# Scatters one per step, gates behind the row sums, and half blocks on 128 columns of weights, in a gated linear attention with a top-1 router

## The chip, the cores and the metric

The kernel runs on one core of one Trainium2 chip. The metric is the time of one execution on the device in microseconds (us); of several runs the median counts.

## The reference

All arrays are float32. For 4 batches and 8 heads of width 48, over 768 steps:

```python
state = alpha[:, :, t, :, None] * state + np.einsum('bhd,bhe->bhde', k[:, :, t], v[:, :, t])
y[:, :, t] = np.einsum('bhd,bhde->bhe', q[:, :, t], state)
```

The result, as 3072 token rows x of 384 numbers, goes through a router with 8 experts:

```python
logits = (x / norm(x)) @ (expert_emb / norm(expert_emb)).T / tau
expert_idx = argmax(logits); gate_w = softmax(logits)[expert_idx]
h = np.maximum(x[mask] @ w1[e], 0.0)              # w1: 384 x 1024
out[mask] = gate_w[mask, None] * (h @ w2[e])      # w2: 1024 x 384
```

Each token goes through the one expert that it chose.

## The kernel before, in words

**First stage: attention and routing.** The 3072 tokens are 24 chunks of 128 (six for each batch), and a loop at L719 takes one chunk per step, with work of earlier chunks in the same step. Step s loads chunk s + 2 (`load`, L447, on the SP queue), turns its alpha, k and q on TensorE and scans the decays on VectorE (`decays`, L467), scales the queries on POOL (`decay_queries`, L498, the product `qs` at L513), computes the scores of chunk s - 1 (`scores`, L565: 32 matmul records into `sc`, then a causal mask, `masked`, on POOL at L582), adds the state's share and the chunk's own for chunk s - 2 (`mix_states`, `mix_chunk`) and brings chunk s - 3 into rows of tokens (`rows`). `decay_state` (L532) makes `dec` on POOL from the running state, and `end` (L518) is its factor; both are for TensorE's `mix_states` of a later step.

When a group of two to four chunks (GROUPS, L61) has its rows, `choose` finds each token's expert, and `place` (L343) gives every token a row in the table `xs` in DRAM; it appends the group's chunks to the list `send`. `to_rows` (L311) is the indirect DMA from POOL that scatters the 128 rows of one chunk, so there are 24 scatters. L800 sends one or two chunks in a step: two where the list holds more than two. After chunk 15 (S0 - 1) `fetch_early` (L176) reads 256 rows of the first expert back on the SP queue, and the loads of the first expert's weights follow it there. From step 24 on, whatever is in the list is sent at once.

**Second stage: experts.** `run(i)` (L1255) takes expert number i with three blocks of 128 tokens (one in run 0, whose first two blocks are done early). Runs 1 to 7 ("pair") compute the first layer with sums of weights (`mix_first_weights`, on POOL) and sums of rows (`mix_first_rows`, 13 operations on VectorE), in 23 products (`first_layer_blocks`, L1080), and two of the three blocks of the second layer likewise (`second_layer_pair`, L1179), with sums of w2 (`mix_weights`, L1005, on POOL; in run 1 on VectorE). Run i also prepares the gates of run i + 1: `begin_gates` (L944, five small operations on VectorE, the first one is `gtop`), then the squares, the norm and the end. For run 0, `prepare_gates` does all that. The fetch of run i + 2's rows (`xg`) is issued at the head of run i.

After each run, `run_extra` (L1319) reads how many tokens of the expert are left over; if there are some, `half_block` (L1223) takes 64 of them. Its first layer goes over 8 groups of 128 columns of w1 and over three 128-row parts of the contraction; each of the 24 pairs of those is two matmuls with 64 columns of weights (`i`), which write the lower and the upper 64 partitions of the PSUM tile `pyo`. With this input three of the eight experts run their half block.

**What sets the order.** A scheduler in front of the kernel orders each engine's instructions by itself, unless the kernel says otherwise: `tc.issue_after(x)` puts what is issued inside it behind x. `behind(s)` (L460) stands behind the last VectorE and POOL operation of `decay_queries` of step s. `turn_of(calls)` (L874) stands behind all of the list; `by_dve` (L988) chains VectorE calls through the list `dve`. At the head of a pair's run, `dve` is empty.

Of the kernel before, what the change touches and what calls it, by code (L numbers as in the profile page):

```python
# [12 lines left out]
ALU = mybir.AluOpType  # L13
# [14 lines left out]
def kernel(  # L28
# [12 lines left out]
    nc = tc.nc  # L41
# [3 lines left out]
    P = 128  # L45
# [4 lines left out]
    NS = N // P  # L50
    KT = DM // P
# [144 lines left out]

    def in_turn():
        return tc.issue_after(last["pe"].ins) if last else ExitStack()


    with ExitStack() as c1:
# [296 lines left out]
        def decay_queries(s):  # L498
            c = s % NCH
            d = st[s]  # L500
            L = NP * P
            pa, r = d["a"]
            rv = r.rearrange("p (n t) -> p n t", t=P)
            ini = ini_s[s % 2]
            nc.vector.reciprocal(
                ini.rearrange("p (n t) -> p n t", t=P)[:, :, 0:1], rv[:, :, 0:1]
            )
            a = work.tile([P, L], FP32, name="a")
            d["a_scan"] = by_dve = nc.vector.tensor_tensor_scan(  # L509
                a, pa, ini, 0.0, ALU.mult, ALU.add  # L510
            )
            d["qs"] = qs = work.tile([P, NP, P], FP32, name="qs", bufs=4)
            by_pool = nc.gpsimd.tensor_tensor(  # L513
                qs.rearrange("p n t -> p (n t)"), d["qc"], a, ALU.mult
            )
            if c > 0:
                d["end"] = end = work.tile([P, NP, 1], FP32, name="end", bufs=3)
                nc.gpsimd.tensor_tensor(end, rv[:, :, 0:1], al0[:, :, s : s + 1], ALU.mult)  # L518
            d["last"] = by_dve, by_pool

        def keys_back(s, ps=ps_tr, tag="tr"):
# [10 lines left out]
        def decay_state(s):  # L532

            if s % NCH == 0:
                return
            d = st[s]
            dec = d["dec"] = work.tile([P, NP, DP], FP32, name="dec", bufs=3)
            nc.gpsimd.tensor_tensor(
                dec, carried["state"], d["end"].to_broadcast([P, NP, DP]), ALU.mult
            )  # L540

# [174 lines left out]
        a0 = prepare_loads()  # L716
        prepare_fills()
        load(1)
        for s in range(NS + 3):  # L719
            if s + 2 <= NS:  # L720
                v_last = load(s + 2)
            if s + 2 == NS:

                with tc.issue_after(v_last.ins):
                    weights(0)
            if 0 <= s - 1 < NS:
                with in_turn():
                    keys_back(s - 1)
            if s < NS:
                decays(s)  # L730
            if s == NS:
                with in_turn():
                    turn_early()
            copied = None
            if s < NS:
                placing(s)
            if 3 <= s <= NS:
                with in_turn():
                    copied = rows(s - 3)
            if s < NS:  # L740
                queries(s, copied)
                decay_queries(s)
            if 0 <= s - 1 < NS:
                decay_state(s - 1)

                with in_turn(), tc.issue_after(st[s]["a_scan"].ins) if s < NS else ExitStack():
                    scores(s - 1)
            if s == 0:
                with behind(s), in_turn():
                    prepare_first(a0)  # L750
                with behind(s):
                    prepare_logits()
            if NS <= s < NS + 2:
                with in_turn():
                    first_layer_early(2 * (s - NS), 2 * (s - NS) + 1)
            if 0 <= s - 2 < NS:
                with in_turn():
                    mix_states(s - 2)
                with in_turn():
                    mix_chunk(s - 2)  # L760
            if 0 <= s - 1 < NS:

                with in_turn(), tc.issue_after(st[s]["a_scan"].ins) if s < NS else ExitStack():
                    update(s - 1)
            if 0 < s < NS and s % NCH == 0:

                with in_turn():
                    keys_back(s, ps_mm, "mm")
            if NS <= s < NS + 2:
                with in_turn():  # L770
                    first_layer_early(2 * (s - NS) + 1, 2 * (s - NS) + 2)
            if NS <= s < NS + 2:
                with in_turn():
                    rows(s - 2)
            if s == 1:
                with in_turn():
                    turn_logits()
            if s == 2:
                with behind(s):
                    routing_constants()  # L780
            if s == 3:
                with behind(s):
                    convert_constants()
            if 4 <= s < 4 + NXG * (NC + 1):
                i, t = divmod(s - 4, NC + 1)
                with behind(s):
                    nc.gpsimd.memset(xg_s[i][:, t], 0.0)
            if s == 3:
                with behind(s):
                    nc.gpsimd.memset(blank, 0.0)  # L790

            if s >= NS:
                n = placing(s)
            if lead:
                with tc.issue_after(st[s - 1]["dve"].ins):
                    next(lead[0])
                if s == S0 + 5:
                    lead.pop()
            with behind(s) if s < NS else tc.issue_after(st[NS - 1]["masked"].ins):
                n_now = len(send) if s >= NS else 0 if s == NS - 1 else 1 + (len(send) > 2)  # L800
                for c in send[:n_now]:
                    to_rows(dest[:, c : c + 1], x_g[group_of[c]][:, c - GROUPS[group_of[c]][0]])
                    send.remove(c)
                    if c == S0 - 1:
                        fetch_early()
            if s == NS:
                with tc.issue_after(st[NS - 1]["masked"].ins):
                    nc.gpsimd.memset(w1_s[1][:, 0, 0:1], 0.0)
                weights(1)
            for r in rows_of(s):  # L810
                g = group_of[r]
                if r == GROUPS[g][1] - 1:
                    with tc.issue_after(st[min(s, NS) - 1]["dve"].ins):
                        choose(g)
                    with behind(s) if s < NS else ExitStack():
                        nc.gpsimd.tensor_copy(x_g[g][:, :, TK], toks[:, slice(*GROUPS[g])])
            if s > NS:
                with in_turn():
                    first_layer_early(2 * (s - NS) + 2, 2 * (s - NS) + 4)
# [7 lines left out]
    with ExitStack() as c3:  # L827
# [42 lines left out]
            return ins  # L870

        pe = []

        def turn_of(calls):  # L874
            queue = ExitStack()
            for call in calls:
                queue.enter_context(tc.issue_after(call.ins))
            return queue

        def turn(xg, xT, n, by=None):  # L880

# [101 lines left out]

        dve = []

        act = []

        def by_dve(call, *args, **kwargs):  # L988
# [65 lines left out]
        def mix_first_rows(i):  # L1054
# [20 lines left out]
            for to, a, b, op in (  # L1075
                (15, 3, 5, ALU.subtract), (10, 0, 3, ALU.add), (16, 0, 1, ALU.add),
            ):
                v.tensor_tensor(x[to], x[a], x[b], op)

        def first_layer_blocks(w1_t, xT, hT, between, squares):  # L1080

# [141 lines left out]
        def half_block(w1_t, w2_t, xT, gate, col):  # L1223

            hT = hp.tile([P, FT, HALF], FP32, name="hT_half", bufs=1)
            for f0 in range(0, FT, 4):
                ph = ps_y.tile([P, DM], FP32, name="pyo")[:, 0 : 4 * HALF]

                for f in range(4):
                    for k in range(KT):  # L1230
                        for i in range(2):
                            c0 = (f0 + f) * P + i * HALF
                            nc.tensor.matmul(
                                ph[i * HALF : (i + 1) * HALF, f * HALF : (f + 1) * HALF],
                                lhsT=w1_t[:, k, c0 : c0 + HALF], rhs=xT[:, k],
                                start=(k == 0), stop=(k == KT - 1), skip_group_check=True,
                            )
                nc.scalar.activation(
                    hT[:, f0 : f0 + 4].rearrange("p f t -> p (f t)"), ph, AF.Relu
                )  # L1240
# [14 lines left out]
        def run(i):  # L1255
# [8 lines left out]
            if pair:  # L1264
                if i == 1:
                    mix_weights(w2_t, lambda *args: by_dve(nc.vector.tensor_tensor, *args))
                else:
                    mix_weights(w2_t, nc.gpsimd.tensor_tensor)
                left, late = list(range(len(nxt))), list(range(len(nxt)))
                if nxt:  # L1270
                    known = begin_gates(i + 1, by_dve)

# [21 lines left out]
            if nxt:  # L1294
                if pair:
                    mix_first_weights(i + 1, nc.gpsimd.tensor_tensor)
                with turn_of(dve):
                    mix_first_rows(i + 1)
            if nxt and not pair:
                with tc.issue_after(done.ins), tc.issue_after(turned.ins):  # L1300
                    prepare_gates(i + 1)
            if not nxt:

                with turn_of(done_pair):
# [2 lines left out]
            for t in range(2 if pair else 0, blocks_run(i)):  # L1307
                sent = second_layer(
                    w2_t, hT[:, :, t * P : (t + 1) * P], gate[:, t : t + 1], col[:, t : t + 1],
                    (lambda *args: by_act(nc.scalar.mul, *args)) if pair  # L1310
                    else nc.vector.tensor_scalar_mul,
                )
            if not pair:

# [114 lines left out]
```

## Time and profile before

| | |
|---|---|
| median of three runs | 415.48 us (415.04, 415.48, 420.29) |
| profiled execution, its own time | 416.3 us |
| its span, first to last instruction | 414.6 us |
| mean granted TensorE clock | 0.988 |
| DMA packets | 119,539, 60.26 MB |
| the 24 scatters on POOL (L312) | 1009 ns each on the mean |
| loads of weights to TensorE in the half blocks (L1233) | 288 records, mean 138 ns |
| matmuls of the half blocks' first layer (L1233) | 288 records, 9.9 us busy |

How to read the lines: a timeline row has the start in the span, the length (both us), the engine, the line of the kernel, the operation, output<-inputs, the shape of the tile and the count of merged instructions; in brackets stands the idle time of the engine before it and what ended it. PE is TensorE's matmuls, PEld its loads of weights, which overlap with them; DVE is VectorE, ACT ScalarE, POOL GpSimd, SP the queue that issues the plain DMAs. A float32 matmul of the code shows as two matmul records and two load records. In the clock row, each digit is the granted TensorE clock in one of 40 equal slices of the span, in tenths.

### The profile page before, as it was taken

To read this page: it belongs to the slowest core of one execution; us is meant where nothing else is said; L and a number is where in the kernel's file an instruction comes from. 1 tells how busy PE (TensorE), PEld (TensorE's weight loads), DVE (VectorE), ACT (ScalarE), POOL (GpSimd) and SP (SyncE) were. 2 spreads that over 40 slices of the span, in tenths; PEclk is the share of its full clock that TensorE was granted. 3 is DMA by queue.
4 is the path that set the end of the run, shared out by engine and by line. 5 is a ranking of instruction groups with operands and counts; after the bars stand their busy time and mean duration, and the time that the engine had idled before them with its cause. 6 is when DMAs were issued, how large, how long until landed. Compare 5 with 4: busy or idle time off the path is not lost. (4 is left out here: it accounts for less than half of the span.)

```text
span 414.6 us, 12189 instructions
## 1 busy us (share of the span) xinstructions
PE 398.9 (96%) x4688; PEld 354.6 (86%) x4688; DVE 259.3 (63%) x655; ACT 205.4 (50%) x516; POOL 252.7 (61%) x344
## 2 busy tenths in 40 slices
PE   8999999999999989999999999999999999899994
PEld 8889989888898768588979979989979979879974
DVE  4999979788889514792583572680582375374640
ACT  3455545554455532653673753662672482492520
POOL 6365687677766434771837939937837755946301
PEclk9999999999999996999999999999999999999998
DMA  9999999998986992495802903703800910100101
GB/s 140 155 166 155 155 185 188 195 193 157 191 174 125 344 371 86 136 344 180 290 16 68 344 19 115 291 19 94 315 20 21 337 50 19 40 2 16 40 16 45
DMA packets 119539, 60.26 MB, mean 145 GB/s; under 512 B 102447, under 2 KB 113976, under 8 KB 119472
## 3 DMA queue, kind: packets, MB, share of 16 engines
q1 hardware_dynamic: 115368, 49.15, 50.2%
q0 software_dynamic: 3728, 10.16, 6.9%
q8 instruction: 44, 0.72, 0.7%
q14 instruction: 23, 0.19, 0.2%
q10 hardware_dynamic: 376, 0.05, 0.1%
HBM read 49.69 MB, written 11.45 MB: 147 GB/s over the span
## 5 line engine op out<-in xcount | busy, mean ns | idle before, releaser
L990 DVE TENSOR_TENSOR hT<-hT,pq 128x384 f32<-128x384 f32 x84 | 45.5, 553 | 50.9 <-PE pq L1098 31.3
L860 POOL DMA_INDIRECT out_dram<-y,sx x25 | 24.6, 983 | 65.9 <-ACT y L995 42.4
L513 POOL TENSOR_TENSOR qs<-qc,a 128x512 f32<-128x512 f32 x24 | 30.6, 1276 | 37.0 <-DVE a L509 15.9
L1098 PE MATMUL pq<-xT_m,w_m 128*128 128x192 f32 x252 | 45.4, 326 | 0.0
L973 PE MATMUL pyo<-w,hT 128*128 128x384 f32 x128 | 42.6, 486 | 0.0
L1098 PEld LDWEIGHTS pq<-xT_m,w_m 128*128 128x128 f32 x252 | 40.8, 190 | 0.0
L973 PEld LDWEIGHTS pyo<-w,hT 128*128 128x128 f32 x128 | 24.0, 190 | 14.8
L312 POOL DMA_INDIRECT xs<-x,dest x24 | 24.2, 1009 | 17.8 <-DVE x L656 10.1
L480 DVE TENSOR_TENSOR_SCAN r<-pa,inr 128x511 f32<-128x511 f32 x24 | 29.2, 1216 | 9.0 <-PE pa L195 8.6
L995 ACT ACTIVATE hT<-hT 128x384 f32<-128x384 f32 x56 | 28.4, 518 | 12.2 <-DVE hT L990 9.6
L1010 POOL TENSOR_TENSOR w_m<-w 128x768 f32<-128x768 f32 x12 | 22.6, 1883 | 17.4 <-PE pq L1195 17.4
L1052 POOL TENSOR_TENSOR w_m<-w,w_m 128x256 f32<-128x256 f32 x42 | 30.1, 729 | 3.8 <-PE pq L1098 2.4
L192 PE MATMUL sc<-qs,kr 64*64 64x128 f32 x768 | 29.4, 273 | 2.1 <-issue 2.1
L509 DVE TENSOR_TENSOR_SCAN a<-pa,ini 128x512 f32<-128x512 f32 x24 | 29.3, 1223 | 1.1
L1195 PE MATMUL pq<-w_m,hT_m 128*128 128x192 f32 x168 | 28.5, 327 | 0.2 <-issue 0.2
L1052 POOL TENSOR_TENSOR w_m<-w 128x256 f32<-128x256 f32 x36 | 26.3, 742 | 3.7 <-PE pq L1098 2.4
L1195 PEld LDWEIGHTS pq<-w_m,hT_m 128*128 128x128 f32 x168 | 27.4, 190 | 0.5 <-issue 0.5
L192 PEld LDWEIGHTS sc<-qs,kr 64*64 64x64 f32 x768 | 22.7, 134 | 4.6 <-issue 4.2
L192 PE MATMUL pyx<-sm,vt 128*64 128x128 f32 x384 | 26.3, 279 | 0.0
L652 ACT COPY lg<-pyx 128x32 f32<-128x32 f32 x24 | 4.4, 185 | 40.8 <-PE px L192 34.7
L192 PEld LDWEIGHTS pyx<-sm,vt 128*64 128x64 f32 x384 | 20.5, 136 | 4.1 <-issue 3.6
L624 ACT COPY ycols<-pyx 128x256 f32<-128x256 f32 x48 | 17.9, 377 | 9.4 <-PE pyx L192 5.9
(230 smaller groups left out, 1003.6 us busy)
## 6 DMA issues: line engine op xcount, KB each, us to landing
w<-in_moe_w_dram SPq DMA_DIRECT2D x12, 1536.0 KB
kt<-in_k_dram SPq DMA_DIRECT2D x24, 192.0 KB
qt<-in_q_dram SPq DMA_DIRECT2D x24, 192.0 KB
vt<-in_v_dram SPq DMA_DIRECT2D x24, 192.0 KB
xg<-xs SPq DMA_DIRECT2D x22, 196.5 KB
at<-in_alpha_dram SPq DMA_DIRECT2D x24, 168.0 KB
w<-in_moe_w_dram SPq DMA_DIRECT2D x6, 512.0 KB
w<-in_moe_w_dram SPq DMA_DIRECT2D x8, 384.0 KB
```

Source lines behind the costliest of these rows:

```text
L192: last["pe"] = nc.tensor.matmul(*args, **kwargs)
L312: ins = nc.gpsimd.indirect_dma_start(out=xs, out_offset=bass.IndirectOffsetOnAxis(ap=rows, axis=0), in_=x, in_offset=None, bounds_check=E ...
L480: nc.vector.tensor_tensor_scan(r[:, L - 2 :: -1], pa[:, L - 1 : 0 : -1], inr[:, L - 2 :: -1], 1.0, ALU.mult, ALU.add,)
L509: d["a_scan"] = by_dve = nc.vector.tensor_tensor_scan(a, pa, ini, 0.0, ALU.mult, ALU.add)
L513: by_pool = nc.gpsimd.tensor_tensor(qs.rearrange("p n t -> p (n t)"), d["qc"], a, ALU.mult)
L860: ins = nc.gpsimd.indirect_dma_start(out=out, out_offset=bass.IndirectOffsetOnAxis(ap=col, axis=0), in_=y, in_offset=None, bounds_check=N - 1,
L973: pe[:] = [nc.tensor.matmul(py, lhsT=hT[:, f], rhs=w2_t[:, f], start=(f == 0), stop=(f == FT - 1),)]
L990: dve[:] = [call(*args, **kwargs)]
L995: act[:] = [call(*args, **kwargs)]
L1052: by(w[to], w[x], w[y], op)
L1098: pe[:] = [nc.tensor.matmul(to[:, f], lhsT=w[left][:, f * P : (f + 1) * P], rhs=x[right], start=start and f == 0, stop=stop, skip_group_ch ...
L1195: pe[:] = [nc.tensor.matmul(to, lhsT=left[:, f], rhs=right[:, f], start=start and f == 0, stop=stop and f == n - 1, skip_group_check=True,)]
```

## The change

Four edits:

1. Scatters: at most one chunk is sent at the old place of each step before 23; steps 18 and 20 (`s - 1` in TWO = (17, 19)) send one more at the head of the step, on POOL behind the mask of chunk s - 2 and behind the last `end` or `dec` of chunks s - 2 and s - 1. From step 24 on the rest is sent as before.
2. Gates: the last operation of `mix_first_rows`, of run 0's `prepare_gates` and of the run's third block (run 0's one block) is kept in `before_dve`, and the chain `dve` of the next pair's run begins behind them.
3. w2's sums (`mix_weights`) are issued ahead of that, so that they aren't held by it.
4. Half blocks: one matmul with 128 columns of weights in place of two with 64.

```diff
+        TWO = (S0 + 1, S0 + 3)
+
+        def send_next():
+            c = send.pop(0)
+            to_rows(dest[:, c : c + 1], x_g[group_of[c]][:, c - GROUPS[group_of[c]][0]])
+            if c == S0 - 1:
+                fetch_early()
+
         for s in range(NS + 3):
+            if s - 1 in TWO:
+                with turn_of([st[s - 2]["masked"]] + [d["by"] for d in (st[s - 2], st[s - 1]) if "by" in d]):
+                    send_next()
...
             with behind(s) if s < NS else tc.issue_after(st[NS - 1]["masked"].ins):
-                n_now = len(send) if s >= NS else 0 if s == NS - 1 else 1 + (len(send) > 2)
-                for c in send[:n_now]:
-                    to_rows(dest[:, c : c + 1], x_g[group_of[c]][:, c - GROUPS[group_of[c]][0]])
-                    send.remove(c)
-                    if c == S0 - 1:
-                        fetch_early()
+                for _ in range(len(send) if s >= NS else min(len(send), s < NS - 1)):
+                    send_next()
...
                     for k in range(KT):
-                        for i in range(2):
-                            c0 = (f0 + f) * P + i * HALF
-                            nc.tensor.matmul(
-                                ph[i * HALF : (i + 1) * HALF, f * HALF : (f + 1) * HALF],
-                                lhsT=w1_t[:, k, c0 : c0 + HALF], rhs=xT[:, k],
-                                start=(k == 0), stop=(k == KT - 1), skip_group_check=True,
-                            )
+                        nc.tensor.matmul(
+                            ph[:, f * HALF : (f + 1) * HALF],
+                            lhsT=w1_t[:, k, (f0 + f) * P : (f0 + f + 1) * P], rhs=xT[:, k],
+                            start=(k == 0), stop=(k == KT - 1), skip_group_check=True,
+                        )
...
                 left, late = list(range(len(nxt))), list(range(len(nxt)))
+                dve.extend(before_dve)
                 if nxt:
                     known = begin_gates(i + 1, by_dve)
...
                 with turn_of(dve):
-                    mix_first_rows(i + 1)
+                    before_dve[:] = [mix_first_rows(i + 1)]
             if nxt and not pair:
                 with tc.issue_after(done.ins), tc.issue_after(turned.ins):
-                    prepare_gates(i + 1)
+                    before_dve.append(prepare_gates(i + 1))
...
                     (lambda *args: by_act(nc.scalar.mul, *args)) if pair
-                    else nc.vector.tensor_scalar_mul,
+                    else lambda *args: before_dve.append(nc.vector.tensor_scalar_mul(*args)),
```

`turn_of` moves up in the file, `end` and `dec` are kept under `st[s]["by"]`, and `mix_first_rows` returns its last operation. Lowered, the change leaves the count of operations on VectorE, ScalarE and SP as it is; on POOL, four of the 24 scatters stand elsewhere, and on TensorE every half block has 24 matmuls less. On VectorE the five operations of `begin_gates` move: for run 2's gates from the end of run 0 ahead of its block's y to behind it (three of the five behind the branch of the half block), and for the gates of runs 3 to 7 from ahead of the last sum of a pair's first layer to a place between the first and the second y of the same run's second layer.

More of the change, by code (lines that the diff above doesn't have):

```diff
@@ L198, in in_turn, with turn_of @@
         return tc.issue_after(last["pe"].ins) if last else ExitStack()
+    def turn_of(calls):
+        queue = ExitStack()
+        for call in calls:
+            queue.enter_context(tc.issue_after(call.ins))
+        return queue
     with ExitStack() as c1:
@@ L517, in decay_queries @@
                 d["end"] = end = work.tile([P, NP, 1], FP32, name="end", bufs=3)
-                nc.gpsimd.tensor_tensor(end, rv[:, :, 0:1], al0[:, :, s : s + 1], ALU.mult)
+                d["by"] = nc.gpsimd.tensor_tensor(end, rv[:, :, 0:1], al0[:, :, s : s + 1], ALU.mult)
             d["last"] = by_dve, by_pool
@@ L537, in decay_state @@
             dec = d["dec"] = work.tile([P, NP, DP], FP32, name="dec", bufs=3)
-            nc.gpsimd.tensor_tensor(
+            d["by"] = nc.gpsimd.tensor_tensor(
                 dec, carried["state"], d["end"].to_broadcast([P, NP, DP]), ALU.mult
@@ L872 @@
         pe = []
[L874 to L878, printed above, removed]
         def turn(xg, xT, n, by=None):
@@ L984 @@
         dve = []
+        before_dve = []
         act = []
@@ L1077, in mix_first_rows @@
             ):
-                v.tensor_tensor(x[to], x[a], x[b], op)
+                ins = v.tensor_tensor(x[to], x[a], x[b], op)
+            return ins
         def first_layer_blocks(w1_t, xT, hT, between, squares):
```

## The prediction

> **What bounds the kernel now.** I read the page first: its busy rows and its clock row.
>
> ```profile
> span 414.6 us, 12189 instructions
> PE 398.9 (96%) x4688; PEld 354.6 (86%) x4688; DVE 259.3 (63%) x655; ACT 205.4 (50%) x516; POOL 252.7 (61%) x344
> ...
> PEclk9999999999999996999999999999999999999998
> ```
>
> TensorE is busy for 96% of the span, so time moves mostly if TensorE's own stream gets longer or shorter. The 6 in the clock row covers 155 to 166 us: the stretches view gives a mean clock of 0.75 for 150 to 160 us and 0.90 for 160 to 170 us. Then I read the timeline of the stages that the change touches. First the scatters of token rows; these are POOL's rows around the two that step 12 sends together:
>
> ```profile
> 76.80 1.04 POOL L312 DMA_INDIRECT xs<-x,dest  x1 [0.16 <-issue]
> 78.15 0.98 POOL L312 DMA_INDIRECT xs<-x,dest  x1 [0.30 <-issue]
> 79.13 0.65 POOL L582 TENSOR_SCALAR_AFFINE_SELECT sm<-sm 128x512 f32<-128x512 f32 x1
> ```
>
> and TensorE's rows at that time:
>
> ```profile
> 77.90 0.65 PE L192 MATMUL sc<-qs,kr 64*64 64x128 f32 x10
> 78.93 0.46 PE L192 MATMUL sc<-qs,kr 64*64 64x128 f32 x4 [0.38 <-issue]
> 79.69 0.85 PE L192 MATMUL sc<-qs,kr 64*64 64x128 f32 x18 [0.30 <-issue]
> 80.29 0.58 PE L192 MATMUL pyx<-qs,dec 64*64 64x128 f32 x12
> ```
>
> The 32 score matmuls take 2.39 us until the next group starts (77.90 to 80.29), and stop twice, with no semaphore to blame. In an undisturbed step they run in one piece:
>
> ```profile
> 73.04 1.06 PE L192 MATMUL sc<-qs,kr 64*64 64x128 f32 x32
> 73.92 0.62 PE L192 MATMUL pyx<-qs,dec 64*64 64x128 f32 x16
> ```
>
> That is 0.88 us. So this pair of scatters costs 1.51 us of TensorE. The same reading gives 1.49 at 55.55 us, 0.75 at 101.14 us and 1.22 at 112.16 us: exactly the four steps with two scatters (placed at steps 8, 12, 16, 18), 4.97 us together. The steps with one scatter show no stop in this group but one of about 0.3 us. Why TensorE stops, no row says; the coincidence is four of four.
>
> Second, the half blocks (three of the eight experts run one). Here are the first two:
>
> ```profile
> 189.12 1.62 PE L1233 MATMUL pyo<-xT,w 128*64 128x64 f32 x48
> 191.06 1.75 PE L1233 MATMUL pyo<-xT,w 128*64 128x64 f32 x48 [0.33 <-DVE y L976]
> 192.62 2.83 PE L1246 MATMUL pyo<-w,hT_half 128*64 128x192 f32 x32
> ...
> 282.99 3.27 PE L1233 MATMUL pyo<-xT,w 128*64 128x64 f32 x96
> 286.08 2.79 PE L1246 MATMUL pyo<-w,hT_half 128*64 128x192 f32 x32
> ```
>
> From first row to L1246 the first layer takes 3.50 us, then 3.09 (the third, at 317.57 us, 3.07). Each matmul of the code is two records, so 48 become 96. Matmuls on either side follow without a gap, so a half block stands fully on TensorE's path.
>
> **The change, part by part.** (1) **Scatters.** Nothing is added: the same 24 scatters, each of about 1.0 us on POOL plus 0.3 before it. One each moves from step 8 to 11 and from 12 to 15. From steps 16 to 21 the two pairs become one scatter per step, with an extra, early one at the head of steps 18 and 20. The last early row fetch (SP) still follows the scatter of block 15 at step 21, so SP's queue keeps its order. The early ones stand on POOL behind the mask of the step before, ahead of dec and of qs. Their 1.3 us fit into POOL's idle time there, 1.96 us before the qs of step 18 and 2.33 before that of step 20 (L513's rows at 109.26 and 121.33 us); dec is read by TensorE only in the next step. Cover gone, qs would come up to 1.3 us later, and scores(18) after it, again a step later.
> The gain: pairs of steps 8, 12 and 16 gone, 1.49 + 1.51 + 0.75 = 3.75. The moved scatters cost 0 to 0.3 each as single ones; I take 0.3 for all. The pair of step 18 (1.22) becomes two with the mask (0.65) between them, and step 20 gets a new second one: neither spacing is in the trace. Bounds: all of 1.22 saved and nothing new (-1.2), or nothing saved and as much added (+1.2). I take the middle, 0, nudged to -0.2, since the rows show stops only where scatters touch. Sum -3.6 us, bounds -5.0 to -2.2. It passes through: TensorE waits for no load of q, k or alpha in this stage, and the weights' loads start on SP (134.3 us) only behind the early row fetch, which waits until 133.2 us for that same scatter of block 15.
>
> (2) **Half blocks.** 48 matmuls on 64 columns of weights become 24 on 128; the columns loaded are the same. What counts is how fast weights come in. Loads with 128 columns under matmuls too short to hide them stand in the timeline of the weight loads, at the placing:
>
> ```profile
> 71.96 0.30 PEld L192 LDWEIGHTS pyx<-before,ones 128*128 128x128 f32 x2
> 72.18 0.30 PEld L192 LDWEIGHTS pyx<-chosen,earlier 128*128 128x128 f32 x2
> ```
>
> Two loads start 0.22 us before the next two, 0.11 each, though each matmul streams 32 columns only. In the half block now, a left and a right load of 64 columns run side by side: 3.09 us / 48 pairs = 0.064 per pair. Changed: 24 matmuls are 48 records, each behind a load of 0.11: 48 x 0.11 = 5.28 us. The difference is 1.78 + 2.19 + 2.21 = **+6.2 us**. The 0.33 us wait for DVE's y in the first is inside the 3.50 and vanishes under the longer first half. Here two rules disagree. The Trainium skill, TensorEngine Tiling (Array Packing), Instruction Overhead, charges each matmul some 60 cycles, so half as many matmuls should be cheaper: 96 x 60 cycles fall to 48 x 60, at the 2.4 GHz of its page TensorE: Matmul & The Clock Gate about 1.2 us saved per half block, -3.6 in all. The same page's Key Properties say that tiles load and multiply in parallel, which the change gives up. The rows side with the second: at 0.064 us a pair already takes less than one full load. Lower bound: loads hidden, 48 x 0.064 = 3.09, that is -0.4; upper: loads and matmuls one after the other, 48 x (0.11 + 0.058) = 8.1 us, +14.6. I take 6.2, nearest the measured load. ScalarE's two relus gain slack; PSUM tiles and the second layer stay.
>
> (3) **Gates behind the sums.** In the DVE queue now, five small operations for the gates of the run after next stand too early, and wait for the rows' DMA:
>
> ```profile
> 189.72 0.19 DVE L990 TENSOR_REDUCE gtop<-xg 128x4 f32<-128x32 f32 x1 [2.51 <-DMA xg<-xs]
> ...
> 190.40 0.61 DVE L976 TENSOR_SCALAR y<-pyo,gt 128x384 f32<-128x384 f32 x1
> ```
>
> (1.52 us again at 239.54, 0.89 at 268.63). Changed, they follow the sums of the rows and the first y of a run, about 10 us later, when the rows have landed. They are 0.19 + 0.16 + 0.17 + 0.16 + 0.18 = 0.9 us, and DVE idles 1.6 us before the second y in runs 1, 4 and 5; in runs 2 and 3 only 0.40, but there the removed wait gives it back. Behind them stand the second y, its scatter, then next run's sums. On TensorE the waits showed as the 0.33 us counted above and as a stop at 246.03 us of 0.36 beyond the usual spacing (0.19 shown as idle): **-0.4 us**, bounds -1 to +0.5. w2's sums of run 1 stay ahead of the new order: nothing.
>
> (4) **Code size.** A skipped half block is a jump over (48 + 16) matmuls of two records and two loads each, 256 TensorE instructions; changed it is (24 + 16) x 4 = 160. The waits view has 1.7 us of TensorE idle behind this branch. I take -0.5, bounds -1.7 to +1.
>
> Sum: -3.6 + 6.2 - 0.4 - 0.5 = **+1.7 us** on the profiled execution's 416.3 us (span 414.6): 418.0. That execution stood 0.8 above the median of 415.48, so the median to expect is 417.2.
>
> **The rivals.** *Loads hidden* (half blocks unchanged, TensorE's stream falls): -3.6 - 0.4 - 0.4 - 0.5, about 410.6. For it: in 128-column matmuls elsewhere loads overlap matmuls; against it: those stream 128 or 192 columns, here 64. *The early scatters stop TensorE too*: gain only 2.2, or less, 418.6 to 420.5. For it: they follow a scatter by some 2 us. Against: a mask between. *The clock window missed*: 0.75 and 0.90 above are 2.5 + 1.0 = 3.5 us of TensorE work lost, behind a stretch (152.4 to 154.9) in which TensorE was busy 0.57 of 2.5 us, under four scatters in a row that stay. The skill's TensorE: Matmul & The Clock Gate, Part 1, has free-running windows of some 3.4 us; then a stage shifted by 3.6 us can fall between windows (413.7) or, as now, into one (417.2). The rows show one such event, so I keep it. *Slower*: if in the half blocks the loads can't run under the matmuls (8.1 us each), the sum is +14.6 - 4.5 = +10.1, 425.6. It decides from about 0.15 us per record; 0.11 was measured with loads under short matmuls. *No effect of the spreading at all*: 420.8.
>
> **How the numbers follow.** Likeliest, all parts as worked out, 55%: 417.2, own range 415 to 419.5. Early scatters or no effect of spreading, 14%: up to 420.8. Clock window missed, 12%: 413.7. Loads hidden, 12%: 410.6. Loads in series, 6%: 425.6. Rest 1%. Taking in the hidden loads with some room, and leaving out the last two (7%) and the tails, gives 410 to 421.5. A 2% step is 8.3 us, about what a measurement of this kernel can tell from no change: faster needs hidden loads and a missed window together (407.1), 0.03; slower needs loads in series, or a second clock drop on top of the likeliest sum, 0.08; within, 0.89.
>
> **What would show it.** L1233's successor: 48 records in about 5.3 us before the second layer (right), 3.1 (hidden) or 8 (serial). The score group in one piece of 0.88 us in steps 9, 13, 17 and 19; whether stops appear behind the early scatters in steps 18 to 21. No DVE wait of gtop on the rows' DMA. The 6 in the clock row still there. I am wrong if the half blocks don't grow, or if stops of the score group come back at other steps.

## The result and the profile after

The changed kernel takes **417.91 us** in the median of 16 runs, the kernel before 415.38 us in 16 runs beside it: a ratio of 1.0063, 95% interval 1.0035 to 1.0091, or 2.6 us more. Forecast were 417.2 us and +1.7 us. Ratios here and below leave disturbed runs out, medians don't, and the two can differ by up to a quarter of a per cent.

The page of the changed kernel, with its busy rows and the clock row:

```profile
span 416.3 us, 11902 instructions
PE 400.9 (96%) x4544; PEld 358.0 (86%) x4544; DVE 268.2 (64%) x655; ACT 205.7 (49%) x516; POOL 253.1 (61%) x344
...
PEclk9999999999999989999999999999999999999998
```

TensorE is as full as before, with 144 records fewer and 2.0 us more of busy time. The 6 in the clock row became an 8: the drop to half clock behind the first stage lasts 3.4 us (153.3 to 156.7) where it lasted 6.8 (155.1 to 161.9). What that is worth, and why it isn't the change's doing, comes below.

**First stage.** These are POOL's rows, and then TensorE's, around the step in which step 12's pair of scatters stood before:

```profile
75.44 1.02 POOL L319 DMA_INDIRECT xs<-x,dest  x1 [0.16 <-issue]
76.48 0.64 POOL L589 TENSOR_SCALAR_AFFINE_SELECT sm<-sm 128x512 f32<-128x512 f32 x1
```

```profile
76.84 1.06 PE L192 MATMUL sc<-qs,kr 64*64 64x128 f32 x32
77.72 0.62 PE L192 MATMUL pyx<-qs,dec 64*64 64x128 f32 x16
```

One scatter, and behind it 32 score matmuls in one piece: 0.88 us to the next group, where it was 2.39. In the other three steps (9, 17 and 19) it is 0.94, 0.88 and 0.88. The early scatters of steps 18 and 20 lie here:

```profile
103.70 1.02 POOL L319 DMA_INDIRECT xs<-x,dest  x1
104.74 0.65 POOL L589 TENSOR_SCALAR_AFFINE_SELECT sm<-sm 128x512 f32<-128x512 f32 x1
105.56 1.00 POOL L319 DMA_INDIRECT xs<-x,dest  x1 [0.17 <-issue]
...
114.84 1.03 POOL L319 DMA_INDIRECT xs<-x,dest  x1
```

and the score groups behind them take 1.03 and 1.12 us, 0.15 and 0.24 over the undisturbed 0.88. The last transposes of alpha start at 130.67 us (133.55 before), 2.9 us earlier, although the waits view has a new entry, one stop in step 15 for a load of q:

```profile
PE phe L192 <- DMA w<-in_moe_w_dram: 1.9, 2, 1.3
PE pyx L192 <- ACT ycols L631: 1.7, 1, 1.7
...
PE pq L195 <- DMA qt<-in_q_dram: 1.2, 1, 1.2
```

The same view of the kernel before began with `PE sc L192 <- issue: 2.1, 7, 0.4` and `PE pq L1098 <- PEq L1326: 1.7, 2, 1.3` (the score stops and the jumps over half blocks). Neither entry is left.

**Second stage.** The first half block, on TensorE:

```profile
185.47 5.47 PE L1242 MATMUL pyo<-xT,w 128*128 128x64 f32 x48
190.87 2.82 PE L1255 MATMUL pyo<-w,hT_half 128*64 128x192 f32 x32
193.62 0.59 PE L1109 MATMUL pq<-xT,w 128*128 128x192 f32 x2
```

5.40 us from first row to second layer; the other two (280.58 and 317.55 us) take as long. Before, they took 3.50, 3.09 and 3.07. On VectorE, the first gates of that run no longer wait for the rows:

```profile
185.95 0.19 DVE L1000 TENSOR_REDUCE gtop<-xg 128x4 f32<-128x32 f32 x1
186.06 0.16 DVE L1000 TENSOR_TENSOR xg<-xg,used 128x4 f32<-128x4 f32 x1
193.74 0.41 DVE L1260 TENSOR_SCALAR y<-pyo,gt 64x192 f32<-64x192 f32 x1 [7.53 <-PE pyo L1255]
```

All six `gtop` of the pairs' runs are without a wait; before, three waited 4.9 us together. The stretch from the first `pyo<-w,ehT` to TensorE's last matmul grew from 244.1 to 249.1 us.

### The profile page after: what moved, and what is told of

Its sections match the earlier page's. It is cut to its first block, busy times and chain, and to the rows that moved or that the text cites. A ratio compares the mean times of both kernels' runs of the same rounds, so it can differ in the third digit from the quotient of the medians.

```text
span 416.3 us, 11902 instructions
## 1 busy us (share of the span) xinstructions
PE 400.9 (96%) x4544; PEld 358.0 (86%) x4544; DVE 268.2 (64%) x655; ACT 205.7 (49%) x516; POOL 253.1 (61%) x344
## 5 line engine op out<-in xcount | busy, mean ns | idle before, releaser
L319 POOL DMA_INDIRECT xs<-x,dest x24 | 24.4, 1016 | 16.5 <-DVE x L663 10.8
L1020 POOL TENSOR_TENSOR w_m<-w 128x768 f32<-128x768 f32 x12 | 21.7, 1806 | 20.1 <-PE pq L1206 20.1
L192 PE MATMUL sc<-qs,kr 64*64 64x128 f32 x768 | 27.2, 272 | 0.0
L192 PE MATMUL pyx<-sm,vt 128*64 128x128 f32 x384 | 26.4, 279 | 0.0
L192 PEld LDWEIGHTS pyx<-sm,vt 128*64 128x64 f32 x384 | 20.5, 136 | 4.2 <-issue 3.6
L192 PEld LDWEIGHTS sc<-qs,kr 64*64 64x64 f32 x768 | 21.7, 133 | 1.1 <-issue 0.5
```

What stands on the lines that cost most here:

```text
L192: last["pe"] = nc.tensor.matmul(*args, **kwargs)
L319: ins = nc.gpsimd.indirect_dma_start(out=xs, out_offset=bass.IndirectOffsetOnAxis(ap=rows, axis=0), in_=x, in_offset=None, bounds_check=E ...
```

## The experiments

The kernels come in three groups, each on one chip with the kernel before beside it. The chips differ in pace: the kernel before took 415.6 us on that of e1 to e4, 405.3 on that of e5 to e9 ("the quick chip" below) and 414.3 on that of f1 to f4. So each kernel is judged by its ratio, and differences in us are the ratio times the time of the kernel before there.

| kernel | median us | before there | ratio (95% interval) |
|---|---|---|---|
| e1 all but the half blocks | 415.0 | 415.6 | 0.9976 (0.9947 to 1.0004) |
| e2 scatters alone | 412.57 | 415.6 | 0.9941 (0.9914 to 0.9968) |
| e3 half blocks alone | 421.43 | 415.6 | 1.0155 (1.0083 to 1.0226) |
| e4 half blocks by 32 tokens | 459.12 | 415.6 | 1.1056 (1.0982 to 1.1129) |
| e5 gates alone | 406.22 | 405.29 | 1.0010 (0.9988 to 1.0032) |
| e7 pairs behind the mask | 405.2 | 405.29 | 1.0006 (0.9986 to 1.0026) |
| e8 single scatters later | 412.97 | 405.29 | 1.0192 (1.0163 to 1.0220) |
| e9 half blocks twice | 429.63 | 405.29 | 1.0610 (1.0583 to 1.0637) |
| f1 the change again | 416.95 | 414.27 | 1.0090 (1.0054 to 1.0126) |
| f2 scatters alone again | 410.92 | 414.27 | 0.9916 (0.9889 to 0.9942) |
| f3 half blocks alone again | 420.38 | 414.27 | 1.0159 (1.0108 to 1.0211) |
| f4 pairs behind the mask again | 416.05 | 414.27 | 1.0051 (1.0027 to 1.0075) |

### The parts one by one: e1, e2, e3

e1 is the changed kernel with the old loop of the half blocks:

```diff
-                        nc.tensor.matmul(
-                            ph[:, f * HALF : (f + 1) * HALF],
-                            lhsT=w1_t[:, k, (f0 + f) * P : (f0 + f + 1) * P], rhs=xT[:, k],
+                        for i in range(2):
+                            c0 = (f0 + f) * P + i * HALF
+                            nc.tensor.matmul(
+                                ph[i * HALF : (i + 1) * HALF, f * HALF : (f + 1) * HALF],
+                                lhsT=w1_t[:, k, c0 : c0 + HALF], rhs=xT[:, k],
...
```

> All of the change but the half blocks, which keep two matmuls on 64 columns of weights. Theory (the half blocks cost 6 to 7 us, the rest gains about 4): about 411.3 us, 4 below the kernel before, and the half blocks' first layer back at 3.1 to 3.5 us. Rival (the half blocks cost nothing on the path, and what was gained in the first stage is given back in the second by something else): about 417.9, as the changed kernel.

e2 is e1 without the gates' new place:

```diff
-                dve.extend(before_dve)
```

> The kernel before with only its scatters spread. Theory (two scatters in a row stop TensorE; 3.6 us gained in the first stage and kept): about 411.8 us, the score groups of steps 9, 13, 17 and 19 at 0.88 us each, the whole first stage 3.5 us earlier. Rival (the gain is given back later, at the first expert's weights or at the clock's drop): 414 to 415.4, with the first stage 3.5 us earlier and the second longer by 2 to 3.5.

e3 is the kernel before with the new loop of the half blocks and nothing else.

> The kernel before with only its half blocks on 128 columns of weights. Theory (each of 48 records waits for its load, 0.11 us): 5.3 to 5.4 us per half block in place of 3.1 to 3.5, some +6.3, so about 421.7 us. Rival (loads hidden, the second stage grew for another reason): within 0.5 of the kernel before, 415.4.

**e2** gains 2.5 us (1.3 to 3.6), near the theory. Its first stage is 3.85 us shorter than e3's, which is that of the kernel before, on the same chip: the last transposes of alpha start at 129.54 and 133.39 us. Most of that is kept in the whole time, and the rival that gives all or nearly all of it back later falls. **e3** loses 6.4 us (3.4 to 9.4) with half blocks of 5.47, 5.40 and 5.40 us: as the theory said. **e1** was to come 4 us below the kernel before, and came 1.0 below (interval from -2.2 to +0.2). Its half blocks are back at 2.95 to 3.12 us, so the half blocks aren't what is missing; it is e2 plus the gates, and by the ratios the gates cost 1.4 us instead of gaining. That is within the noise of two intervals, but it is the wrong sign, so the gates were run alone.

### What sets the pace of a half block: e4 and e9

e4 cuts every matmul of the half blocks' first layer into two of 32 tokens, with all 128 columns of weights loaded for each. The half blocks' outputs aren't those of the reference there; the loads and the tokens streamed are as many as said.

```diff
-                            ph[:, f * HALF : (f + 1) * HALF],
-                            lhsT=w1_t[:, k, (f0 + f) * P : (f0 + f + 1) * P], rhs=xT[:, k],
+                        for i in range(2):
+                            c0 = f * HALF + i * 32
...
+                                ph[:, c0 : c0 + 32],
+                                lhsT=w1_t[:, k, (f0 + f) * P : (f0 + f + 1) * P],
+                                rhs=xT[:, k, i * 32 : (i + 1) * 32],
...
```

> The changed kernel, with every matmul of the half block's first layer cut in two of 32 tokens: 128 columns of weights are loaded twice as often, and the tokens streamed are as many as before. Theory (the load of weights sets the pace): 96 records at 0.11 us, 10.6 us per half block, so 5.2 more in each of three, about 433.5 us. Rival (the streaming of tokens or the drain sets the pace): half blocks stay at about 5.4 us, 417.9; a fixed cost for each record of 0.05 with streaming for the rest would give some 8 us, 425.7.

It took far more than any of the three: 459.1 us. The row of its first half block, and its table of stretches (us, then each engine's busy time with the records that touch the stretch, the granted clock, the DMA share, GB/s):

```profile
186.52 15.36 PE L1244 MATMUL pyo<-xT,w 128*128 128x32 f32 x96
201.81 4.78 PE L1258 MATMUL pyo<-w,hT_half 128*64 128x192 f32 x32
```

```profile
190.00:192.00 2.00, 2.00 (x20) 2.00 (x20) 0.00 (x0) 0.00 (x1) 0.00 (x0) 1.00 0.03 8
193.00:197.00 4.00, 4.00 (x20) 4.00 (x20) 0.00 (x0) 0.00 (x0) 0.00 (x0) 0.50 0.00 0
```

20 records touch 2 us at full clock and 4 us at half clock. From start to start the records stand 0.112 us apart for the first 5.7 us, and 0.213 apart after that. So the load theory holds where the clock stayed: at 32 tokens a record takes exactly what it takes at 64 (5.40 / 48 = 0.112 in the changed kernel), and halving the tokens changes nothing. What none of the theories expected is the clock: it falls to half 4.2 to 5.7 us into each of the three half blocks and stays there for 13.7 to 17.1 us. The rows of the first and second layers sum to 48.1 + 13.9 us in the three, where the changed kernel has 16.4 + 8.5: 37.1 us more, nearly all of the 41.3 us between the two (43.9 and 2.6 above the kernel before).

e9 computes every product of the half blocks' first layer twice:

```diff
                 for f in range(4):
-                    for k in range(KT):
...
+                    for _ in range(2):
+                        for k in range(KT):
...
```

> The changed kernel, with every product of the half blocks' first layer computed twice: 96 records in place of 48 in three half blocks, and the jump over a half block as long as in the kernel before. Load theory: 96 x 0.1117 = 10.7 us per half block if the clock stays, so 5.4 us more in each, about 434; if the clock drops to half after 5.7 us, as under 32 tokens, 15.3 us in each, about 450. Code size theory: TensorE's stops at the four skipped half blocks grow again, from 0.47 us each to some of 0.8 to 2.1. Rival: they stay at 0.47, and their size before was chance.

```profile
178.96 10.83 PE L1243 MATMUL pyo<-xT,w 128*128 128x64 f32 x96
```

10.8 us in each of the three, at full clock throughout: load theory right, no drop with 64 tokens even over 10.8 us. That isn't a clean comparison with e4, since e9 ran on the quick chip, whose records show fewer drops anyway. That chip is quicker in the old half blocks as well: in e5, e7 and e8 those that wait for nothing take 2.85 us from first row to second layer, where they take 2.87 to 3.19 on the other chips, most of them over 3.0; the new ones keep 0.112 us a record on all three. Its jumps are told with the next point.

### Gates alone, and the jumps over half blocks: e5, with e9 and the rest

e5 is e1 with the old sending of scatters, so the kernel before with the gates' edits alone (2 and 3 of the change).

> The kernel before with only the gates ordered behind the sums of rows. Theory (waits for the rows' DMA in VectorE's queue go): 0.4 to 2 us faster than before, 413.5 to 415, and no stop of TensorE ahead of the products of the second layer in run 1 (246.03 us in the kernel before). Rival (the gates, now later, hold the second y and then the next sums): 1 to 2 us slower, 416.5 to 417.5, with new stops of TensorE at the heads of runs 2 to 6.

It stands at +0.4 us (-0.5 to +1.3): no gain, and not the loss of the rival either. The stop ahead of run 1's second layer, 0.52 us from start to start in the kernel before and 0.64 to 1.47 in e2, e7, e8, f2 and f4, is gone in e5, as in every kernel with the gates' order (e3 and f3, without that order, don't show it either). Yet the waits view of e5 has something else:

```profile
PE pq L1110 <- PEq L1339: 3.6, 2, 2.0
```

L1339 is the jump over a half block that has nothing to do. TensorE's rows at one of them, and the same place of the changed kernel:

```profile
340.91 1.14 PE L1110 MATMUL pq<-xT,w 128*128 128x192 f32 x6
344.00 0.84 PE L1110 MATMUL pq<-xT,w 128*128 128x192 f32 x2 [1.95 <-PEq L1339]
```

```profile
353.53 1.85 PE L1109 MATMUL pq<-xT,w 128*128 128x192 f32 x8
355.22 0.98 PE L1109 MATMUL pq<-xT,w_m 128*128 128x192 f32 x5
```

Four of the skipped half blocks lie between matmuls of the pairs' runs, and at each TensorE stands still. The starts on either side are 0.47 us apart at least. Beyond 4 x 0.47, the ten executions with the long half block (256 TensorE instructions to jump over) lose, together over the four jumps: before 1.45, e1 2.5, e2 1.1, e4 1.5, e5 3.3, e7 0, e8 0.5, e9 3.3, f2 0.4, f4 0.9; on the mean 1.5 us. The four with the short one (160 instructions: after, e3, f1, f3) lose 0 in all sixteen jumps. e9 restores the length and nothing else of the old half block, and has 2.12 and 2.13 us at two of its jumps: the stops go with the length. Whether the distance itself does it, or where the fetched blocks of instructions then begin and end, wasn't separated.

The DMA records of TensorE's instruction fetches show more. Only the second and the third of the four jumps ever stop long. In the ten executions these are 20 jumps, of two kinds. At 13 of them TensorE's starts are 0.80 to 2.28 us apart; there a fetch begins 0.7 to 1.7 us ahead of the stop, the one before it more than 22 us ahead, and TensorE goes on 2.4 to 3.0 us after that late fetch began (in e5 the fetch begins at 341.02 us, and the stop lasts from 341.73 to 344.00). At the other 7 the starts are 0.47 us apart, and there another fetch lies 6.3 to 6.8 us ahead. So the long stops look like a wait for a fetch that was begun late. A fetch is 16.4 KB (0.72 MB in 44 of them), and the Trainium skill, Runtime: NRT & Kernel Launch, Instruction fetch mechanics, makes 256 instructions of such a block and says that a jump to what lies outside the pages held has to wait for its page. 256 is just the length of the old jump.

The four kernels with both the long jump and the gates' order (e1, e4, e5, e9) lose 2.7 us on the mean, the six with the long jump alone 0.7. That would explain e1's and e5's missing gain, but it rests on one execution of each kernel, and e5's is not typical: it took 408.6 us where the median is 406.2, and its clock fell to half for 3.4 us right behind its second stop (344.2 to 347.6 us). Over all of e5's runs the granted clock is 0.9961 on the mean, that of the kernel before on this chip 0.9976; the difference is 0.6 us of TensorE's time, more than the 0.4 that e5 stands above. Why the order on VectorE should matter to TensorE's fetches, no row says; it stays open.

### Why TensorE stops under scatters: e7, e8, and f1 to f4 on another chip

e7 moves both scatters of the four steps behind the mask:

```diff
-                    to_rows(dest[:, c : c + 1], ...
+                    with tc.issue_after(st[s - 1]["masked"].ins) if n_now == 2 and s < NS else ExitStack():
+                        to_rows(dest[:, c : c + 1], ...
```

> The kernel before, with both scatters of the four steps that have two put behind the mask of the same step, so still in a row, but behind the score matmuls and not over them. Theory A (a scatter stops TensorE where it runs over the score matmuls): score groups of steps 9, 13, 17 and 19 at 0.9 us, no stop elsewhere, about 411.8 us. Theory B (two scatters in a row stop it, wherever they are): some 0.75 to 1.5 us of stops in each of the four steps in other matmul groups, 415 to 415.5.

e8 is e2 with each single scatter before step 24 some 0.7 us later, behind four memsets, and the mask behind the scatter:

```diff
-                    send_next()
+                    if s < NS:
+                        for _ in range(4):
+                            fill = nc.gpsimd.memset(filler, 0.0)
+                    with tc.issue_after(fill.ins) if s < NS else ExitStack():
+                        sent_now = send_next()
+                    if s < NS:
+                        with tc.issue_after(sent_now.ins):
+                            mask(s - 1)
...
```

> The kernel with only its scatters spread, with four fillers of 0.2 us on POOL ahead of each single scatter before step 24, and the mask kept behind the scatter, so that each single scatter starts some 0.7 us later and runs over the score matmuls. Theory A (a scatter over the score matmuls stops them): stops of 0.5 to 1.2 us in some 14 score groups, 7 to 16 us more than the 412.6 of the scatters alone, so 419 to 428. Theory B (only two in a row stop TensorE): score groups at 0.9 us, within 1 us of 412.6.

Both failed as tests, and told something else. On this chip e5 has the pairs of scatters in the old places, and its score group is whole. POOL's rows, then TensorE's:

```profile
54.51 1.18 POOL L319 DMA_INDIRECT xs<-x,dest  x1 [0.17 <-issue]
56.00 0.98 POOL L319 DMA_INDIRECT xs<-x,dest  x1 [0.30 <-issue]
```

```profile
55.54 1.06 PE L192 MATMUL sc<-qs,kr 64*64 64x128 f32 x32
56.42 0.62 PE L192 MATMUL pyx<-qs,dec 64*64 64x128 f32 x16
```

0.88 us, with a pair right over it. **The stops that the first term of the prediction removes don't exist on this chip**, so nothing of e7 or e8 can show what makes them. e7's 1.0006 says no more than that. Of e8's 7.8 us, 5.5 are a plain wait that the edit made: the mask now comes too late for the products with v (`PE pyx L192 <- POOL sm L594: 5.5, 8, 1.5` in its waits view).

So the change, the two single parts and e7's kernel were run together once more:

> The changed kernel once more, beside the three next on one chip. The chip of the gates, mask and late-scatter runs ran the kernel before in 405.3 us and showed no stop of the score matmuls where two scatters stand in a row. Theory (the gain of the spreading exists only where a chip stops there): if the kernel before takes about 415, a ratio of 1.005 to 1.009; if it takes about 405, no gain is left to pay for the half blocks and the ratio is 1.010 to 1.014, 4 to 5.5 us more. Rival (the stops come and go by execution, not by chip): 1.006 on either chip.

> The kernel before with only its scatters spread, once more. Theory: 0.990 to 0.995 of the kernel before where that takes about 415, 0.998 to 1.002 where it takes about 405. Rival (stops by execution): 0.994 on either chip.

> The kernel before with only its half blocks changed, once more; its first stage is that of the kernel before, with scatters in pairs. Theory: score groups of steps 9, 13, 17 and 19 at 1.8 to 2.4 us where the kernel before takes about 415, at 0.88 where it takes about 405; 5.4 us per half block on both, and 4.5 to 6.5 us more than the kernel before on both.

> The kernel before with both scatters of a pair behind the mask, once more. Where the kernel before takes about 415: theory A (a scatter over the score matmuls stops them) 411 to 412.5 and no stops; theory B (two in a row stop TensorE wherever they are) 415 to 415.5, with stops of 0.75 to 1.5 us in another group. Where the kernel before takes about 405: within 0.3 % of it, and nothing told apart.

The chip took 414.3 us for the kernel before, and f3, with the old pairs, has the stops again; its score groups take 2.33, 2.26, 1.66 and 2.05 us, against 2.37, 2.39, 1.78 and 2.10 in the kernel before and 2.33, 2.33, 1.77 and 2.08 in e3. They are the same to 0.13 us in three executions on chips that have them. Step 9's group in f3:

```profile
55.56 0.75 PE L192 MATMUL sc<-qs,kr 64*64 64x128 f32 x14
56.57 0.47 PE L192 MATMUL sc<-qs,kr 64*64 64x128 f32 x4 [0.26 <-issue]
57.31 0.69 PE L192 MATMUL sc<-qs,kr 64*64 64x128 f32 x14 [0.28 <-issue]
```

Here f2 gains 3.5 us (2.4 to 4.6), f3 loses 6.6 (4.5 to 8.7), f1, the whole change, 3.7 (2.2 to 5.2; by the medians 2.7). That is what the chip theory said, with f1 at the upper end of its range, f3 0.1 us beyond it and one score group (1.66 us) a little below; the two parts alone sum to 3.1. The groups behind single scatters agree with a difference between chips: from 50 us on and with the last group left out, the longest group of an execution that no pair covers takes 1.11 to 1.33 us in the ten executions elsewhere, and 0.99 to 1.03 in the four on the quick chip. That the stops come by chip and not by execution rests on three chips and on the unknown ones of the first profiles; what differs in the chip isn't shown.

f4 went against both of its theories: 2.1 us slower than the kernel before (1.1 to 3.1), with more stops. I had misread the order. The mask of that moment belongs to the scores of the step before, so the pair moved 0.6 us later and came to lie almost wholly over the score group. POOL's and TensorE's rows in f4:

```profile
54.31 0.64 POOL L582 TENSOR_SCALAR_AFFINE_SELECT sm<-sm 128x512 f32<-128x512 f32 x1
55.12 1.19 POOL L312 DMA_INDIRECT xs<-x,dest  x1 [0.17 <-issue]
56.61 0.97 POOL L312 DMA_INDIRECT xs<-x,dest  x1 [0.30 <-issue]
```

```profile
55.55 0.61 PE L192 MATMUL sc<-qs,kr 64*64 64x128 f32 x12
56.38 0.63 PE L192 MATMUL sc<-qs,kr 64*64 64x128 f32 x10 [0.22 <-issue]
57.17 0.45 PE L192 MATMUL sc<-qs,kr 64*64 64x128 f32 x4 [0.15 <-issue]
57.89 0.50 PE L192 MATMUL sc<-qs,kr 64*64 64x128 f32 x6 [0.27 <-issue]
```

Three stops in place of two; the four groups take 2.85, 2.85, 2.17 and 2.73 us, 7.1 over the undisturbed where f3 has 4.8. So in these two kernels the stops grow with the part of the pair that lies over the score group: theory A, a scatter over the score matmuls, fits better than "two in a row", for which the shift should have cost nothing. ScalarE is held as well: the copy of `lg` that follows the `px` matmuls by 0.27 us in an undisturbed step follows them by 1.90 us in f3's step 9, by 2.43 in f4's and by 0.50 behind f2's single scatter; on the quick chip by 0.27 to 0.40 everywhere. VectorE's scans run on. What holds the two engines isn't in the trace.

## Why the prediction was right, point by point

**Scatters, -3.6 us: right, on such a chip.** Alone they gain 2.5 and 3.5 us, and the first stage shortens by 3.85 (e2 against e3) and 3.13 us (f2 against f3). Every stop that was named is gone, and the early scatters cost some 0.2 us each, about the nothing that was taken. (One reading was short: a last score record of step 16's group starts at 102.85 us, so that pair cost 0.90 and not 0.75.) What the step took for granted is that the stops belong to the kernel. They show on some chips; on the quick one the two executions with pairs have none to remove. Neither the scatters alone nor the changed kernel were run there. e9 is 24.7 us above the kernel before there: the doubling is 16.1 of it, the half blocks' growth on that chip about 3 x (5.40 - 2.85) = 7.6, and 1.0 is left for the jumps (3.3, against an unknown sum in the kernel before there) less whatever the rest of the change gained.

**Half blocks, +6.2 us: right in mechanism and size.** Directly 3 x 5.40 - 9.66 = +6.5 us; alone +6.4 and +6.6. (Those two kernels have the shorter jumps too, so 6.2 - 0.5 was forecast for them; their intervals, 3.4 to 9.4 and 4.5 to 8.7, hold it.) A record takes 0.112 us where 0.110 was read off two loads of the placing. The record's time is the same at 32 and at 64 tokens, so it goes with the columns loaded and not with the tokens streamed. The rule of a fixed price for each matmul, which would have made this part a gain of 3.6 us, is wrong here by 10 us: half as many matmuls, each twice as long.

**Gates, -0.4 us: its waits went, its gain didn't show.** VectorE's 4.9 us of waits and TensorE's stop ahead of run 1's second layer are gone, as written, though that stop is absent with the new half blocks alone as well (e3 and f3). Alone the edit is worth +0.4 us (-0.5 to +1.3). Longer stops at the jumps and a lower clock may have hidden a gain there; that isn't shown. In the changed kernel those jumps are short, and what the gates are worth in it wasn't measured.

**Code size, -0.5 us: the term that was mis-sized.** The ten executions with the long jump lose 1.5 us on the mean more than the four with the short one, from 0 to 3.3; in the profiled pair it is 1.45. The bound of -1.7 held it, the value taken was a third of it.

**The clock window.** The rival said that a shorter first stage can make the drop behind it vanish. The drop lasts 6.8 us in the kernel before and in e4, 3.4 in after, e1, e2 and e3, and is absent in f1, f3, f4 and on the quick chip. e3 and f3 have the first stage of the kernel before, and still a shorter drop or none: the drop comes and goes without a shift of the stage. Each 3.4 us at half clock cost 1.7 us of work, by chance of the execution; that is 1.7 us of luck in the profile after. Over the 43 runs of the kernel before beside each group, the granted clock goes with a quarter of the variance of the times in the first group and with half of it in the third (correlations -0.49 and -0.71), and with none on the quick chip.

**The sum.** The two profiles' spans differ by 1.7 us (416.3 - 414.6), and it is made of this. TensorE's first `pyo<-w,ehT` starts at 161.25 us in place of 164.88, 3.6 earlier: -2.9 from the first stage (with 1.4 already lost to the late q, which no other execution on a chip of this pace shows), -1.7 from the shorter drop, +0.9 from the waits for the first expert's weights (1.0 to 1.9 us in the waits views), a little of the gain given back. The stretch from there to the last matmul grew by 5.0: +6.5 for the half blocks, -1.45 for the jumps and -0.36 for the stop at 246.03 us make 4.7. The tail adds 0.3. That the two spans lie just the forecast's 1.7 apart is in part luck: the shorter drop gave 1.7, and the late q and the waits for weights took 2.3.

## What to carry to other kernels

Where matmuls stream few columns, count what is loaded into the array and not the matmuls: two loads of 64 columns side by side came in 0.064 us, one of 128 columns in 0.112, with 64 tokens streamed under it or 32. Code that is jumped over has a price on the engine that jumps, and it shows in a wait with the sequencer's name. And a stop with no semaphore behind it may belong to the chip: look for it in a second execution on another chip before it is made the first term of a sum; here the version that only spreads the scatters is the best of all, 0.9941 and 0.9916 of the kernel before on two chips. On the third, which shows no such stops, it wasn't run.

## What the runs showed of the hardware that was not expected

- Under loads of 128 columns with 32 tokens streamed, the granted clock fell to 0.50 after 4.2 to 5.7 us of such matmuls, with TensorE busy 100% by its rows, and stayed there for 13.7 to 17.1 us, three times in one execution. With 64 tokens it held for 5.4 us, hardly longer than that, in e3 on the same chip, and for 10.8 us in e9 on the quick one. The Trainium skill, TensorE: Matmul & The Clock Gate, Part 1, ties the clock to a window of activity; here a row that says busy wasn't enough. Whether the tokens or the chip made the difference wasn't separated.
- Scatters issued by POOL held TensorE's score matmuls and ScalarE's next copy, by up to 2 us a step, on some chips and not at all on another, at nearly the same places in each execution that has them.
- Every stretch at half clock that ended before its kernel did lasted a whole multiple of 3.41 us: one (after, e1, e2, e3, e5, f2), two (before, e4), four or five (e4).
- A jump over 256 TensorE instructions cost up to 1.8 us beyond its usual 0.47, over 160 nothing in 16 jumps; where it stopped long, TensorE went on 2.4 to 3.0 us after the start of an instruction fetch that had begun just ahead of the jump.
